# Attention and feed-forward in one kernel: the builder's slack for work between score pairs halved

## Chip, cores, metric

One core of a Trainium2 chip. The metric is the device time of one execution in microseconds, the median of several.

## The reference, cut to what matters

```python
x = A_x                                            # 1 x 2048 x 512, bf16
g = sigmoid((x * gate_w).sum(-1, keepdims=True))
a = attention(x, wqkv, wo)                         # 32 heads of 16: softmax(q k^T / 4) v, then @ wo
b = (silu(x @ w_gate) * (x @ w_up)) @ w_down       # feed-forward, inner width 1792
return g * a + (1 - g) * b
```

## The kernel before

The attention scores need 32 x 2048 x 2048 exponentials. They are made in tiles of 128 x 512 ("scores"). Most go in pairs: two TensorE matmuls fill one of two PSUM buffers `s_t`, ScalarE's exponential reads both at once and writes `e_t`. In 72 blocks of four, VectorE computes the exponential instead (`d_t` to `y_t` and on). Between two pairs, TensorE does other work in a "gap": output groups (probabilities times values: `o_ps`, or `x_ps` for VectorE's late blocks), and side pieces of two matmuls each (projections `qp`, `kp`, `vp`, feed-forward `gp`, `up`, `dps`, final projection `a_ps`).

The order on every engine is fixed when the kernel is built, by a loop that keeps a model clock for each engine (`plan.pe`, `plan.act`, `plan.dve`). Cut to what matters, with comments added:

```python
def emit_pair(bs):                       # one score pair and its exponential
    ...
    spend("R", 1 if (bs[0] - bs[1]) % 2 else 2, s_end[i])        # 0.216 us, after s_end
    act(out=e_t[:], in_=s_t[:], func=ACT.Exp, scale=inv_sqrt_dh)
    plan.act = max(plan.act, plan.pe + 0.27) + 0.905
    s_end[i] = plan.act + 0.18           # this buffer is free again
    ...
def spend(mode, mms, ready=0.0):         # 0.1 us for a change of matmul mode
    plan.pe = max(plan.pe + (0.1 if mode != plan.mode else 0.0), ready) + (0.226 if mode == "F" else 0.216) * mms
    plan.mode = mode

def side(most):                          # the next side piece, if it fits
    ...
    if t is None or t > plan.pe + 0.1 or 0.226 * mms + (0.1 if plan.mode != "F" else 0.0) > most:
        return None
    return c

SLACK = 0.2
...
while nxt < nb:
    ...
    room = s_end[pairs[0] % 2] - plan.pe             # until the next pair's buffer is free
    if room > 0.02:
        if to_vector() and not d_wait and d_end[0] <= plan.pe + 0.05:
            ...                                      # a d_t score for VectorE goes first
        n_pv = pvs_ready(plan.pe)
        switch = 0.0 if plan.mode == "C" else 0.1
        fits = int((room + SLACK - switch) / 0.216)  # how many output groups fit
        crowded = pairs[0] - min(e_left.values(), default=pairs[0]) >= EB - 4
        c = side(room + SLACK)
        if n_pv and fits > 0 and (plan.mode == "C" or n_pv > 1 and fits > 1 and (pv_turn[0] or c is None)
                                  or crowded or c is None and fits == 1):
            emit_pv(); ...; continue
        if c is not None:
            pace.credit -= emit_piece(c); ...; continue
    ...
    emit_pair(list(range(nxt, min(nxt + 2, nb))))
    nxt += 2
```

A VectorE block's output group counts as ready 0.4 us after the model clock says that the block ends (`late.append((plan.dve + 0.4, mine))`).

Of the kernel before, what the change touches and what calls it, by code (L numbers as in the profile page):

```python
# [78 lines left out]
def kernel(  # L79
# [995 lines left out]
    def side(most):  # L1075

        due = any(not c.out() for n in range(plan.slot, plan.slot + 12) for c in need.get(n, []))
        c = pace.next(plan.slot) if pace.credit > 0 or due else None
        if c is None:
            return None  # L1080
        mms, _, takes = c.pieces[c.i]
        t = m_ready() if takes else 0.0
# [3 lines that stand above are left out]
# [3 lines left out]
            pay_v() if vops else pay_d() if d_wait else pay()  # L1089
        emit_pv()  # L1090

    SLACK = 0.2
    def to_vector():

        un, at_ = divmod(nxt, 4 * KT)
        if vcur:
            if nxt % 4 in [b % 4 for b in vcur["b"]]:
                return 0
            return 2 if at_ >= 4 * KT - 4 * (NV - vcur["i"]) else 1
        if nxt < 16 or at_ > (50 if un < UNITS - 1 else 12) or y_live[0] >= 3 or sum(v[0] for v in vops) > 6:  # L1100
            return 0
        return 1

    while nxt < nb:
# [12 lines left out]
        if room > 0.02:  # L1117
# [6 lines left out]
            switch = 0.0 if plan.mode == "C" else 0.1  # L1124
            fits = int((room + SLACK - switch) / 0.216)
# [3 lines that stand above are left out]
# [105 lines left out]
```

## Time and profile before

| | before |
|---|---|
| median time | 872.0 us |
| span in the profile | 869.8 us |
| ScalarE, TensorE, VectorE busy | 97%, 92%, 92% |
| exponentials on ScalarE | 880, mean record 1.09 us |
| score tiles on VectorE | 288 |

ScalarE is the bound. A **start pitch** is the distance between the starts of two exponentials that follow one another with nothing between; there are 822 such pairs among 880 exponentials. An **end pitch** is the distance between their ends, start plus duration of the record. "Excess" is the sum of what lies over the commonest pitch.

### The profile page before, as it was taken

Reading aid. Unit: us, or ns where it says so; the run is one execution under the profiler, and the core shown is the slowest. Engines: PE = TensorE matmul, PEld = TensorE weight load, DVE = VectorE, ACT = ScalarE, POOL = GpSimd, SP = SyncE. Lnnn points to the kernel's source line nnn. Section 1 sums busy time; section 2 is a strip of 40 time slices with the busy share of each in tenths; the row PEclk is TensorE's granted clock in tenths of the full one; section 3 lists DMA queues with packets and bytes.
Section 4 is the critical chain, followed back from the end, with each engine's and each line's share of the span. In section 5 each row is a group of like instructions: output and inputs, shape, how many; then the busy total and the mean of one; then the engine's idle time right before and its main releaser. Section 6 shows DMA issues by size and latency. Waiting matters only on the chain.

```text
span 869.8 us, 14419 instructions
## 1 busy us (share of the span) xinstructions
PE 798.7 (92%) x5232; PEld 208.8 (24%) x5232; DVE 796.5 (92%) x1117; ACT 842.7 (97%) x944; POOL 8.6 (1%) x31
## 2 busy tenths in 40 slices
PE   5999999999999999999999989989998989889985
PEld 2222222222222222222222222222222222222221
DVE  7889999999999999999999999989999999998974
ACT  3999999999999999999999999999999999999995
POOL 3000000000000000000000000000000000000000
PEclk9999999999999999999999999999999999999999
DMA  8400011111210012211000122110001121100000
GB/s 200 122 1 10 11 38 43 37 41 35 60 31 8 10 42 66 56 50 41 4 6 18 41 49 61 50 35 13 7 17 41 36 61 36 28 10 4 5 20 25
DMA packets 88064, 31.99 MB, mean 37 GB/s; under 512 B 75648, under 2 KB 87544, under 8 KB 87992
## 3 DMA queue, kind: packets, MB, share of 16 engines
q1 hardware_dynamic: 86408, 30.87, 14.5%
q8 instruction: 41, 0.67, 0.3%
q10 hardware_dynamic: 1584, 0.20, 0.1%
q14 instruction: 31, 0.25, 0.1%
HBM read 20.83 MB, written 2.34 MB: 27 GB/s over the span
## 4 chain that ended last, share of the span: by engine, by line
PE 46%; ACT 35%; DVE 8%; issue 8%; SPq 1%; DMA 1%; DVEq 0%; ACTq 0%
ACT e_t L161 33%; PE s_t L158 17%; PE o_ps L158 9%; PE dps L158 5%; PE d_t L158 4%; DVE y_t L167 4%; PE gp L158 3%; ACT th L161 3%; PE up L158 2%; DVE u_t L167 2%; PE a_ps L158 1%; PE qp L158 1%; PE vp L158 1%; PE kp L158 1%; PE x_ps L158 1%
## 5 line engine op out<-in xcount | busy, mean ns | idle before, releaser
L161 ACT ACTIVATE e_t<-s_t 128x1024 bf16<-128x1024 f32 x880 | 819.6, 1090 | 5.4 <-PE s_t L158 4.8
L158 PE MATMUL s_t<-qx,kaug 64*128 64x512 bf16 x1648 | 326.7, 384 | 47.7 <-ACT e_t L161 44.6
L167 DVE TENSOR_SCALAR y_t<-d_t 128x512 uint16<-128x512 f32 x288 | 197.8, 687 | 28.3 <-PE d_t L158 24.5
L158 PEld LDWEIGHTS <-kaug 64*128 64x128 bf16 x2048 | 99.6, 93 | 377.4 <-issue 374.3
L158 PE MATMUL o_ps<-e_t,vaug 128*32 128x512 bf16 x1760 | 172.0, 387 | 0.7 <-ACT e_t L161 0.7
L158 PE MATMUL d_t<-qx,kaug 64*128 64x512 bf16 x272 | 102.5, 377 | 0.6 <-DVE y_t L167 0.6
L167 DVE TENSOR_TENSOR y_t<-y_t,u_t 128x2048 uint16<-128x2048 uint16 x72 | 87.8, 1219 | 1.0
L167 DVE TENSOR_TENSOR u_t<-u_t 128x2048 f16<-128x2048 f16 x72 | 87.6, 1217 | 0.7
L167 DVE TENSOR_TENSOR u_t<-u_t,z_t 128x2048 f16<-128x2048 f16 x72 | 87.6, 1217 | 0.4
L158 PEld LDWEIGHTS <-vaug 128*32 128x32 bf16 x2048 | 45.1, 94 | 133.1 <-issue 130.2
L158 PE MATMUL dps<-wd_t,mt 128*128 128x512 bf16 x224 | 67.8, 384 | 0.0
L158 PE MATMUL gp<-xT,wg 128*128 128x512 bf16 x224 | 67.8, 384 | 0.0
L158 PE MATMUL up<-xT,wu 128*128 128x512 bf16 x224 | 64.7, 383 | 0.0
L167 DVE TENSOR_SCALAR y_t<-y_t 128x2048 uint16<-128x2048 uint16 x72 | 49.5, 688 | 1.2
L167 DVE TENSOR_SCALAR u_t<-z_t 128x2048 f16<-128x2048 uint16 x72 | 49.5, 687 | 0.8
L167 DVE TENSOR_SCALAR z_t<-y_t 128x2048 uint16<-128x2048 uint16 x72 | 49.3, 684 | 0.2
L167 DVE SCALAR_TENSOR_TENSOR mt<-gs,up 128x512 bf16<-128x512 bf16 x56 | 38.2, 682 | 4.7 <-PE up L158 3.4
L167 DVE SCALAR_TENSOR_TENSOR gs<-th,gp 128x512 bf16<-128x512 bf16 x56 | 38.2, 682 | 2.6 <-ACT th L161 2.3
L161 ACT ACTIVATE th<-gp 128x512 bf16<-128x512 f32 x56 | 36.7, 655 | 0.0
L158 PEld LDWEIGHTS <-mt 128*128 128x128 bf16 x263 | 16.2, 99 | 43.2 <-issue 35.1
L158 PE MATMUL s_t<-on,kaug 64*128 64x512 bf16 x112 | 22.4, 383 | 1.8 <-ACT e_t L161 1.4
L158 PEld LDWEIGHTS <-wu 128*128 128x128 bf16 x224 | 14.2, 97 | 30.1 <-issue 24.7
(104 smaller groups left out, 358.0 us busy)
## 6 DMA issues: line engine op xcount, KB each, us to landing
wg<-in_B_w_gate_dram SPq DMA_DIRECT2D x56, 128.0 KB
wu<-in_B_w_up_dram SPq DMA_DIRECT2D x56, 128.0 KB
on<-osb SPq DMA_DIRECT2D x120, 16.0 KB
rb<-rr SPq DMA_DIRECT2D x15, 128.0 KB
wd_t<-in_B_w_down_dram SPq DMA_DIRECT2D x1, 1792.0 KB
qx<-qst SPq DMA_DIRECT2D x112, 16.0 KB
out_dram<-o_t SPq DMA_DIRECT2D x12, 128.0 KB
kaug<-on SPq DMA_DIRECT2D x20, 64.0 KB
```

What stands on the lines that cost most here:

```text
L158: ordered(nc.tensor.matmul(*args, **kw))
L161: ordered(nc.scalar.activation(*args, **kw))
L167: return lambda *a, **kw: ordered(f(*a, **kw))
```

## The change

So far a side piece and an output group could share one gap and overrun it. The intent is to stop that: work may pass the moment at which the next score buffer is free only by what still leaves the next exponential on time.

```diff
-    SLACK = 0.2
+    SLACK = 0.1
     def to_vector():
```

## The prediction

> **What bounds the kernel now.** I read the page first: busy shares, then the costliest groups.
>
> ```profile
> PE 798.7 (92%) x5232; PEld 208.8 (24%) x5232; DVE 796.5 (92%) x1117; ACT 842.7 (97%) x944; POOL 8.6 (1%) x31
> ...
> L161 ACT ACTIVATE e_t<-s_t 128x1024 bf16<-128x1024 f32 x880 | 819.6, 1090 | 5.4 <-PE s_t L158 4.8
> L158 PE MATMUL s_t<-qx,kaug 64*128 64x512 bf16 x1648 | 326.7, 384 | 47.7 <-ACT e_t L161 44.6
> L167 DVE TENSOR_SCALAR y_t<-d_t 128x512 uint16<-128x512 f32 x288 | 197.8, 687 | 28.3 <-PE d_t L158 24.5
> ```
>
> ScalarE is the bound: 880 exponentials, each over one pair of score matmuls, 97% busy with only 5.4 us of visible idle in front of them. TensorE is nearly as full, but 44.6 us of its idle is a wait for an exponential to free a score buffer (there are two): it has room. The other part of the softmax, 288 single score tiles (d_t), is exponentiated on VectorE in 72 blocks of four.
>
> 97% looks like nothing is left, but an exponential's record lasts 1.09 us on average and 880 of them fill only 819.6 us, 0.93 each: the records overlap. So an exponential can start up to 0.18 us late with no idle shown. I therefore went to the timeline, at a place where one gap between two score pairs holds a side piece (two gp matmuls, one step of the feed-forward part) and an output group (o_ps, probabilities times values). First TensorE alone:
>
> ```profile
> 643.32 0.39 PE L158 MATMUL s_t<-qx,kaug 64*128 64x512 bf16 x2
> 644.20 0.39 PE L158 MATMUL s_t<-qx,kaug 64*128 64x512 bf16 x2 [0.49 <-ACT e_t L161]
> 644.52 0.60 PE L158 MATMUL gp<-xT,wg 128*128 128x512 bf16 x2
> 645.06 0.40 PE L158 MATMUL o_ps<-e_t,vaug 128*32 128x512 bf16 x3
> 645.39 0.39 PE L158 MATMUL s_t<-qx,kaug 64*128 64x512 bf16 x2
> 645.71 0.60 PE L158 MATMUL gp<-xT,wg 128*128 128x512 bf16 x2
> 646.25 0.39 PE L158 MATMUL s_t<-qx,kaug 64*128 64x512 bf16 x2
> ```
>
> Then ScalarE over the same stretch, three narrow windows:
>
> ```profile
> 643.97 1.09 ACT L161 ACTIVATE e_t<-s_t 128x1024 bf16<-128x1024 f32 x1
> ```
> ```profile
> 644.88 1.10 ACT L161 ACTIVATE e_t<-s_t 128x1024 bf16<-128x1024 f32 x1
> ```
> ```profile
> 645.88 1.02 ACT L161 ACTIVATE e_t<-s_t 128x1024 bf16<-128x1024 f32 x1
> ```
>
> Starts 643.97, 644.88, 645.88: the pitch is 0.91, then 1.00. The exponential fed by the pair at 645.39 started 0.49 after that pair, 0.1 late, and its record still overlaps the one before (644.88 + 1.10 = 645.98). That lateness is what the change is after, and the waits do not list it.
>
> **How much of it there is.** I went through the whole trace in the same way: for each exponential, its distance from the one before, and what TensorE did between the two score pairs. Where no other activation lies between (822 of 879), the commonest distance is 0.903 us, and never less. Everything above 0.903, summed, is 19.9 us: all that perfect feeding could gain. By content of the gap (output groups, side pieces, d = a d_t score):
>
> ```
> gap holds            gaps  mean pitch ns  over 925 ns  excess us
> side + 1 group         48      1042            40         6.7
> side + 2 groups        13      1000             6         1.3
> d + 2 groups           55       947            32         2.4
> d + side               73       922            24         1.4
> 3 groups               18       996             8         1.7
> 2 side pieces          21       946             7         0.9
> one side              243       911             2         1.9
> 2 groups              106       910             2         0.7
> d + 1 group           106       909             1         0.6
> nothing / d alone  77/ 40   907/916             0/1       0.8
> ```
>
> Eleven pitches reach 1.2 us (stalls behind VectorE, not late feeding); single excesses over 0.3 us are 1.8 of the 6.7 us in the first row and about 6 us overall.
>
> **What the Trainium skill says.** (1) "Perfetto Trace Analysis", section Optimizing Scalar/DVE Operations: ScalarE pays about 51 ns per instruction on PSUM; with 0.833 ns per element from "ScalarE: Activation LUTs", section What ACT_TABLE_LOAD costs, 1024 elements make an estimate of 853 + 51 = 904 ns. The trace agrees: 903. So 0.903 is a floor that this change cannot move. (2) "TensorEngine Tiling (Array Packing)", section Key Properties: changing the tiling mode drains TensorE. Scores run in 64-row mode, output groups in 32-column mode, side pieces in full mode. Agrees: pair to side takes 0.32 (644.20 to 644.52), the side's two matmuls and the next switch 0.54, group and switch 0.33. (3) "TensorE: Matmul & The Clock Gate", section Back-to-back issue gap: about 216 ns for 512 columns; so each of those steps is matmuls at 0.216 plus about 0.1 for a switch. The change saves switches on an engine that isn't the bound.
>
> **The change part by part.** Only the instruction order changes; the kernel's builder runs a model clock, and SLACK says how far past the moment at which the next score buffer falls free (its s_end) work may run.
>
> How late may a pair be? In the trace the earliest pair starts about 0.05 us after the end of the exponential two before. The shortest pair-start to exponential-start is 0.49. Two pitches are 1.806; minus the record of 1.085 and minus 0.49 leaves 0.23 after that end, 0.18 after the earliest start. So a gap is free up to a pair-to-pair time of 0.903 + 0.18 = 1.08. Contents, with the steps above: side 0.86; two groups 0.87; three groups, d + side and d + two groups all about 1.08, on the edge; side + group 1.19, late by 0.11. The rows of the table follow this.
>
> In the builder's figures: after a pair the room is 0.905 - 0.216 = 0.689; a side with its switch takes 0.552 and leaves 0.137; a group with a switch needs 0.316. 0.137 + 0.2 admits it, 0.137 + 0.1 does not. Third groups (0.157 + slack against 0.216) and d + side (0.473 + slack against 0.552) pass with 0.1 too, but only where the pair before was on time; with 0.2 they also pass behind a late pair. A shared gap stays only where the room is long (after one of the 56 tanh activations).
>
> Removed: (a) shared gaps, 6.7 less the 1.8 us of large stalls: 4.8 us. (b) half of the small excess of side + two groups (0.8) and of two sides (0.9): 0.8 us. (c) a third of the small excess of d + two groups (1.9), d + side (1.4), three groups (0.3): 1.2 us; the others stay, being admitted still. Together 6.8 us.
>
> Added: about 60 to 70 groups move to other gaps, in twos, some 30 gaps. 117 gaps are empty or hold a d alone. A two-group gap costs 7 ns over the floor, 0.2 us in all; some 20 become edge gaps at 30 ns, 0.6 us. One more microsecond for groups forced out when the ring of 12 exponential tiles fills and for chance collisions with VectorE. Together 1.8 us.
>
> Sum: 872.0 - 6.8 + 1.8 = **867.0 us**, 0.6% faster.
>
> **The rivals.**
> 1. TensorE hasn't the gaps: unsharing makes a backlog and groups are forced out late in the ring's last moment. For it: TensorE is 95.9% busy between 200 and 400 us, and waits for exponentials just 112 times. Against it: that busy share contains about 0.1 of switch per step, of which unsharing saves one per gap, and in each 100 us there are 8 to 18 gaps empty or with d alone against 5 to 13 shared. If half the groups came out late by about 0.2 us, 6 us would be lost again: 872 to 875.
> 2. VectorE takes fewer blocks: the builder gives it a score tile when its clock is free, and its own work is 92% busy. A shorter run has less VectorE time; one block fewer means two more exponentials, 1.8 us. For it: a saving of 6 us is most of one block's time (on the page's durations 4 x 0.69 + 3 x 0.69 + 3 x 1.22 = 8.5 us). Against it: VectorE waits 24.5 us for d_t scores, and those get into a gap first. One or two blocks fewer: 869 to 871; one more: 865.
> 3. The lateness costs nothing, because something else ends the run. For it: just 5.4 us of ScalarE idle is shown. Against it: ScalarE is in an unbroken row from 18 to 860 us and nothing catches up a late start. Time then: 872.
>
> **Range and chances.** The mechanism is counted, so the centre lies near the sum; rivals 1 and 2 pull upward by 2 to 5 us, and a full success of all the removable small excess (13 us less what stays at the edge) would give 863. Range 862.8 to 871.0. To be faster by 2% takes 17.4 us of the 19.9 in existence, stalls included: 1%. Slower by 2% takes a backlog much beyond rival 1: 2%. Within 2%: 97%.
>
> **What would show it right or wrong.** Right: side + group gaps fall from 55 (7 of them beside a tanh) to under 10; pitches over 925 ns from 127 to under 70; excess over 0.903 from 19.9 to about 15 us; still 880 exponentials, give or take 4; matmul counts unchanged; the wait of s_t for e_t rises above 46 us. Wrong: shared gaps gone but as many late pitches with three groups or d + two groups (rival 1); 882 or 884 exponentials and fewer than 288 d_t conversions (rival 2); pitches shorter but the same span (rival 3). Large VectorE stalls that shift by chance, 6 us in all, are the largest thing that I can't compute.

## The result, and the profile after

The changed kernel takes 868.99 us (867.87 to 870.62, 4 runs) against 872.01 us (871.86 to 873.24, 4 runs). The ratio is 0.9964, 95% interval 0.9944 to 0.9984: 0.36% faster, within the 2% that counts as the same. (A ratio is the mean of one kernel's fast runs over the mean of the other's in the same rounds, so not quite the ratio of the medians.) The time lies in the predicted range; the gain is 3.0 us where 5.0 was forecast.

The page after, the lines that answer those shown of before:

```profile
PE 789.8 (91%) x5145; PEld 217.3 (25%) x5232; DVE 797.3 (92%) x1120; ACT 842.4 (97%) x944; POOL 8.6 (1%) x31
...
L161 ACT ACTIVATE e_t<-s_t 128x1024 bf16<-128x1024 f32 x880 | 823.3, 1143 | 3.2 <-PE s_t L158 2.4
L158 PE MATMUL s_t<-qx,kaug 64*128 64x512 bf16 x1648 | 332.2, 384 | 43.6 <-ACT e_t L161 38.3
L167 DVE TENSOR_SCALAR y_t<-d_t 128x512 uint16<-128x512 f32 x288 | 198.0, 687 | 30.7 <-PE d_t L158 26.9
```

The same instructions: 880 exponentials, 288 tiles on VectorE (87 of 5232 matmul records are missing from this trace; the second profile of the same kernel, below, has all). The surprise is in the exponentials' line. An exponential's record now lasts 1.143 us, where it was 1.090. The exponential did not become slower: more of them ran closely one behind the other. Counted from the two traces, gap by gap:

```
                                     before   after
gaps with one side + one group           55       2
start pitches over 925 ns               127     121
excess of starts over 0.903 us         19.9    17.4
  of which side + one group             6.7     0.0
           d + side                     1.4     3.9
           d + two groups               2.4     3.4
           two groups                   0.7     2.2
           three groups                 1.7     1.9
excess of ends over 0.917 us            7.5     5.0
  of which single ones over 0.1 us      6.9     4.6   (20 and 19 of them)
```

So the shared gaps went, as predicted, and their 6.7 us with them, and yet hardly fewer starts are late: other rows grew. The time follows the last part of the table, not the first.

**Why ends and not starts.** Take the prediction's own three ScalarE lines. The starts are 643.97, 644.88 and 645.88, and the third seems 0.1 late. But the ends are 643.97 + 1.09 = 645.06, 644.88 + 1.10 = 645.98 and 645.88 + 1.02 = 646.90: 0.92 apart, both times. The late start cost nothing. Its record is just shorter. The kernel after shows the other half of it, in five narrow windows of ScalarE's timeline; each line is two overlapping exponentials, with the start of the first and the time to the end of the second:

```profile
588.17 2.09 ACT L161 ACTIVATE e_t<-s_t 128x1024 bf16<-128x1024 f32 x2
```
```profile
589.08 2.10 ACT L161 ACTIVATE e_t<-s_t 128x1024 bf16<-128x1024 f32 x2
```
```profile
589.98 2.12 ACT L161 ACTIVATE e_t<-s_t 128x1024 bf16<-128x1024 f32 x2
```
```profile
590.88 2.13 ACT L161 ACTIVATE e_t<-s_t 128x1024 bf16<-128x1024 f32 x2
```
```profile
591.79 2.14 ACT L161 ACTIVATE e_t<-s_t 128x1024 bf16<-128x1024 f32 x2
```

Starts: 0.91, 0.90, 0.90, 0.91 apart. Ends (590.26, 591.18, 592.10, 593.01, 593.93): 0.92 apart. Over the trace of before, 537 starts on time stand 0.9033 us apart on average while their ends stand 0.9167 apart (915 to 918 ns for nine in ten), and each record is 0.013 us longer than the one before it. A record that follows idle time is 1.018 us long; the longest is 1.258 us here and 1.316 in the kernel after. So starts run ahead of the work by up to 0.3 us, and whatever a record has over 1.018 us is a store: a late start draws on it first, and only what goes beyond is lost. The traces bear this out gap by gap. Of the 131 starts of before that are over 0.02 us late, 68 are late by less than the record before them has in store: 3.8 us of lateness in sum, and none of their ends is more than 0.002 us late. In the kernel after it is 93 of 125, 6.8 us of lateness, again at no cost. ScalarE's floor for these exponentials is 0.917 us, not 0.903.

By ends, all that better feeding could still gain in the kernel before was 7.5 us, nearly all of it in 20 stalls of over 0.1 us. The difference in the traces adds up: the spans differ by 1.9 us (869.8 and 867.9), the excess of ends by 2.5, and the first exponential came 0.65 later in this profile of after.

### The profile page after: what moved, and what is told of

Its sections match the earlier page's. It is cut to its first block, busy times and chain, and to the rows that moved or that the text cites. A ratio compares the mean times of both kernels' runs of the same rounds, so it can differ in the third digit from the quotient of the medians.

```text
span 867.9 us, 14339 instructions
## 1 busy us (share of the span) xinstructions
PE 789.8 (91%) x5145; PEld 217.3 (25%) x5232; DVE 797.3 (92%) x1120; ACT 842.4 (97%) x944; POOL 8.6 (1%) x31
## 4 chain that ended last, share of the span: by engine, by line
ACT 40%; PE 38%; DVE 10%; issue 9%; SPq 1%; DMA 1%; DVEq 0%; ACTq 0%
ACT e_t L161 37%; PE s_t L158 15%; PE o_ps L158 7%; PE d_t L158 4%; DVE y_t L167 4%; PE dps L158 3%; ACT th L161 3%; PE gp L158 3%; DVE u_t L167 3%; PE up L158 2%; PE vp L158 1%; PE kp L158 1%; DVE mt L167 1%; PE x_ps L158 1%; SPq L174 1%
## 5 line engine op out<-in xcount | busy, mean ns | idle before, releaser
L158 PE MATMUL s_t<-qx,kaug 64*128 64x512 bf16 x1648 | 332.2, 384 | 43.6 <-ACT e_t L161 38.3
L158 PEld LDWEIGHTS <-kaug 64*128 64x128 bf16 x2048 | 109.4, 93 | 381.2 <-issue 377.3
L158 PE MATMUL dps<-wd_t,mt 128*128 128x512 bf16 x205 | 63.5, 384 | 2.5 <-issue 2.5
L158 PE MATMUL gp<-xT,wg 128*128 128x512 bf16 x202 | 62.9, 384 | 2.4 <-issue 2.4
L158 PE MATMUL up<-xT,wu 128*128 128x512 bf16 x205 | 60.9, 383 | 2.1 <-issue 2.1
L161 ACT ACTIVATE th<-gp 128x512 bf16<-128x512 f32 x56 | 40.7, 727 | 0.0
L167 DVE TENSOR_TENSOR osb<-of,x_ps 128x512 bf16<-128x512 f32 x30 | 20.4, 680 | 1.2 <-PE x_ps L158 1.2
```

Of the source, the lines that this page charges most:

```text
L158: ordered(nc.tensor.matmul(*args, **kw))
L161: ordered(nc.scalar.activation(*args, **kw))
L167: return lambda *a, **kw: ordered(f(*a, **kw))
```

## The experiments

Twelve runs were made, on three chips; the times of the kernel before were 872.26 (7 runs), 872.16 (9) and 872.05 (7). Two theories after the result: **starts** (each late start is lost, as predicted) and **stalls** (the floor is 0.917 by ends; what costs are the few stalls that outrun the store, most of them, it says, with TensorE waiting in order for VectorE).

### Half of each side piece dropped, order kept

```diff
 # gate/up, and in the same way the q, k, v, down and final projections
-                for dc in (2 * h, 2 * h + 1):
+                for dc in (0 if h == 0 else DC - 1,):
                     mm(ps[:, :], lhsT=w[:, dc, :], ...)
```

Their outputs are wrong, which doesn't matter for the times. Once on the kernel before:

> The kernel before with half of the matmuls of each side piece dropped (one 512-column matmul left of two; wrong result on purpose), the order of what remains and the builder's model clock untouched. A side piece then takes about 0.22 us less, so a gap with side and group takes about 0.97 and no pair is late. Theory 1 (the prediction's): ScalarE's floor is the start-to-start pitch of 0.903 us and each late start is lost; then some 13 to 14 of the 19.9 us of excess go and the time is 858 to 860. Theory 2: the floor is the end-to-end pitch of 0.917 us (the records grow by 0.013 per exponential while starts are on time, and shrink again at a late start); then only 7.5 us lay above the floor, almost all in 20 large stalls, and the time is 865 to 869, with records of exponentials longer than before (over 1.15 us on average).

and once on the changed one:

> The same dropping of matmuls in the changed kernel (SLACK 0.1). Theory 1: the same 858 to 860 as the thinned kernel before. Theory 2: 864 to 868, i.e. at the most 5 us under the changed kernel; the two thinned kernels differ by less than 2 us, as feeding is no longer in question.

Measured: 870.94 us (868.32 to 872.81; ratio to before 0.9984, interval 0.9962 to 1.0006) and 872.47 us (870.82 to 873.53; 1.0008, 0.9991 to 1.0024). The starts theory wanted 858 to 860 and is refuted. The stalls theory was also too low: 865 to 869 and 864 to 868. TensorE certainly got its room; on the thinned kernel before:

```profile
PE s_t L158 <- ACT e_t L161: 104.9, 332, 1.0
```

It waits 104.9 us for exponentials (before: 46.0). In 702 of 878 cases the pair starts within 0.06 us of its buffer coming free (before: 307), and the records average 1.181 us, but ends stay 0.917 apart. That is the floor, shown with feeding out of the way. What remains over it, 6.8 us, sits where it sat before: stalls at 145.7, 277, 411.9, 460.1, 555.7, 670.4, 682.3, 825.8 us, the same places to 1 us as in the kernel before, most of them smaller. The rest of the miss is new: this profile has three 3.4 us windows at half TensorE clock inside the exponentials (the other: four), where before had one; 2.6 us (3.9 us) of the excess lies in them or just behind. The thinned TensorE was busy for 84% and 85% of the span instead of 92%, and its clock was lowered more often (mean granted clock 0.993 and 0.991, before 0.996). That the one brings the other is not shown, but it confounds these two runs' times, not their floor.

### Slack 0.1 for one kind of work alone

```diff
-            fits = int((room + SLACK - switch) / 0.216)
+            fits = int((room + 0.1 - switch) / 0.216)        # groups_only
-            c = side(room + SLACK)
+            c = side(room + 0.1)                             # sides_only
```

> Slack 0.1 for output groups alone, 0.2 still for side pieces. Side and group then share no short gap. Theory 1: the shared gaps were 4.8 of the 6.8 us to be had, so this is most of the change: 868 to 869.5. Theory 2: small lateness was free, only which large stalls happen to occur matters: anywhere from 867 to 873, without order between the variants of slack, and the excess of ends over 0.917 explains the time to within 0.5 us.

Measured: 870.67 us, ratio 0.9982 (0.9967 to 0.9997). Gaps with one side and one group: 5 beside no tanh (48 before). So with the shared gaps gone the time falls by 0.2%, less than the starts theory wanted; it looks like about half of the change's gain, but the interval overlaps that of the changed kernel (0.9954 to 0.9984). The excess of ends is 5.4 us, 2.1 less than before; the first exponential came 1.4 us later, and the spans differ by 0.7 us, so the ends account for it.

> Slack 0.1 for side pieces alone, 0.2 for output groups. Behind a side a group is again admitted, so shared gaps stay near before's; the builder's TensorE clock ends 3.3 us past ScalarE's, so some pieces are left for the end. Tail 2 to 3 us longer, 872 to 875; the gain of the change is not in this half.

Measured: 881.23 us (1.0104, 1.0083 to 1.0125), 6 us over what was expected. The tail after the last exponential is 12.4 us as foreseen (9.7 before), but the excess of ends doubled to 15.0 us: shared gaps rose (88 without a tanh), side pieces fell behind, and six stalls of over 1 us appeared (the kernel before has none); among TensorE's waits is one for a bound that stands behind its projection on VectorE (`bp` for `aq`, three times, 3.3 us). So the slack for side pieces alone did harm, and the gain does not lie in this half alone.

### The changed kernel again

> The changed kernel once more, for the scatter between chips and to see whether its large stalls sit at the same places: 868 to 870.5. If they are properties of the order (VectorE behind the builder's clock), most of the stalls over 0.1 us of the first profile are there again within 1 us of the same time; if they are chance, they are elsewhere.

Measured: 868.99 us, ratio 0.9969 (0.9954 to 0.9984). It was run at another time. Its stalls stand where the first profile had them: 247, 278, 287, 371, 500, 603, 724, 752, 817 us, within about 1 us and of the same size. So most stalls belong to the order of instructions, not to chance. An exception is one of 1.45 us at 21.6 us, inside a half-clock window that the first profile did not have; the first had four in or behind a half-clock window at 843 us instead, 1.4 us together. That the excess of ends is 4.99 us here and 4.98 there is therefore partly luck.

What makes these stalls is still a VectorE block's output group in half of the cases. One of them in this profile:

```profile
286.22 0.40 PE L158 MATMUL x_ps<-y_t,vaug 128*32 128x512 bf16 x4 [0.52 <-DVE y_t L167]
...
286.76 0.39 PE L158 MATMUL s_t<-qx,kaug 64*128 64x512 bf16 x2
...
287.26 1.02 ACT L161 ACTIVATE e_t<-s_t 128x1024 bf16<-128x1024 f32 x1 [0.32 <-PE s_t L158]
```

Counted in the traces: in the kernel before, the gap just ahead of the late pair holds such a group in 8 of the 20 stalls, 3.8 of their 6.9 us; here in 8 of 16, 2.1 of 4.6 us. TensorE waits for `y_t` before such groups as long as it did (3.1 and 3.0 us in sum), but less of it reaches ScalarE.

The wait of score pairs for exponentials is 38.9 us in this complete trace: it fell from 46.0, where the prediction had it rise.

### VectorE made faster, order kept

```diff
-                (1.26, lambda: vec.tensor_tensor(out=ua, in0=ua, in1=ua, op=ALU.mult)),
+                (1.26, lambda: vec.tensor_tensor(out=uh, in0=uh, in1=uh, op=ALU.mult)),   # 1024 columns of 2048
 # and the same for the two that follow
```

> The kernel before, every engine's instruction order unchanged, but the three 2048-column multiplications and additions of each VectorE block cover 1024 columns (wrong result on purpose): VectorE has some 1.8 us less work per block, TensorE and ScalarE the same. Theory V (the time above ScalarE's floor lies in the stalls in which TensorE, in order, waits for a VectorE block, a gated product or a d_t buffer; five of the largest in the profile of before, 0.43 to 0.85 us, show such a wait just ahead): these stalls go, the excess of ends over 0.917 falls from 7.5 to under 3.5 us, the time is 867 to 868.5. Theory F (late feeding by TensorE itself is what costs): no change, 871.5 to 873.

Measured: 870.12 us, ratio 0.9977 (0.9965 to 0.999). (The result, wrong, still passed the comparison.) Between the two theories. The excess of ends is still some 6.6 us, where under 3.5 was expected, because a half-clock window at 19.9 us, which the profile of before does not have, brings 1.9 us. Outside half-clock windows it fell from 6.4 to 3.6 us; the stalls at 461, 671 and 825 us are gone. Those at 147.7, 414.4, 557.3 and 683.7 us remain, and their lines say why. First the kernel before, all engines:

```profile
144.12 0.69 DVE L167 TENSOR_SCALAR y_t<-y_t 128x2048 uint16<-128x2048 uint16 x1
...
144.86 0.40 PE L158 MATMUL o_ps<-y_t,vaug 128*32 128x512 bf16 x4 [0.47 <-DVE y_t L167]
145.19 0.39 PE L158 MATMUL s_t<-qx,kaug 64*128 64x512 bf16 x2
...
145.68 1.02 ACT L161 ACTIVATE e_t<-s_t 128x1024 bf16<-128x1024 f32 x1 [0.44 <-PE s_t L158]
```

TensorE stands before a VectorE block's output group; the next score pair is behind it in the queue, and ScalarE runs dry. Then the same place with the faster VectorE:

```profile
145.49 0.69 DVE L167 CAST on<-kp 128x512 bf16<-128x512 f32 x1 [2.10 <-PE kp L158]
...
146.09 0.68 DVE L167 TENSOR_SCALAR y_t<-y_t 128x2048 uint16<-128x2048 uint16 x1
...
146.83 0.40 PE L158 MATMUL o_ps<-y_t,vaug 128*32 128x512 bf16 x4 [0.47 <-DVE y_t L167]
147.16 0.39 PE L158 MATMUL s_t<-qx,kaug 64*128 64x512 bf16 x2
...
147.66 1.02 ACT L161 ACTIVATE e_t<-s_t 128x1024 bf16<-128x1024 f32 x1 [0.44 <-PE s_t L158]
```

VectorE now sits idle for 2.10 us before a copy of `kp`, for which it waits on TensorE; the last step of the block is queued behind that copy; TensorE waits for the block. This stall is made by the order on two engines, and the faster VectorE did not remove it. In sum VectorE's speed explains part of the stalls (2.8 us); such an interlock is shown for this one, and the other three have a VectorE block's group just ahead of the late pair too.

### A later ready time for VectorE's blocks

```diff
-                                late.append((plan.dve + 0.4, mine)))),
+                                late.append((plan.dve + 1.0, mine)))),
```

> Slack 0.2 as before, but the builder takes the output group of a VectorE block as ready 1.0 us after its model clock instead of 0.4. Theory V: TensorE no longer waits at o_ps or x_ps for y_t, 868 to 870.5, with a correct result and without touching the shared gaps (some 50 still there). Theory F: no gain, 871.5 to 873.

> Slack 0.1 and the ready time of 1.0 us together. Theory V: waits for y_t gone here too, 866.5 to 869, and the difference to slack 0.2 with the same ready time is under 1.5 us. Theory F: the same time as the changed kernel, 869, and 3 us under slack 0.2.

Measured: 869.91 us at slack 0.2 (0.9969, 0.9957 to 0.9982), 870.05 us at slack 0.1 (0.9975, 0.9961 to 0.9989). At slack 0.2 most of the change's gain appears with its shared gaps all still there (72 of any kind, before 67). So a gain of this size does not need the shared gaps to go. (That it was not theirs in the change is read from their ends, below.) The two gains do not add: slack 0.1 with the later time is no faster than either alone. The waits for `y_t` did not vanish, as I had expected, but went from 2.5 and 0.6 us (`o_ps`, `x_ps`) to 1.3 and 0.4 us at slack 0.2. In the changed kernel they are 0.7 and 2.3 us, no less in sum, so shorter waits are not how the change gained.

### ScalarE's clock in the builder corrected

```diff
-        plan.act = max(plan.act, plan.pe + 0.27) + 0.905
-        s_end[i] = plan.act + 0.18
+        plan.act = max(plan.act + 0.917, plan.pe + 1.288)
+        s_end[i] = plan.act + 0.05
 # e_end, tanh and its reader in the same way; SLACK 0.15
```

> The builder's ScalarE clock as the profile shows it: an end follows an end by 0.917 us, or a pair's issue end by 1.288 us; a score buffer is free 0.05 us after the end; slack 0.15. The builder then lays 73 VectorE blocks and 878 exponentials instead of 72 and 880. Two exponentials fewer are 1.8 us. If the floor of ends is right: 866 to 870; if the floor of starts were right, the builder would leave ScalarE waiting and the time would be over 873.

Measured: 869.1 us, ratio 0.9965 (0.9952 to 0.9977), 878 exponentials. The floor is two exponentials lower, but the excess of ends is 6.6 us: the new order has stalls of its own. No faster than the change.

### Other values of slack

> Slack 0.15, 880 exponentials, nothing left for the end. Late feeding theory: between before and after, 870 to 871. Stalls theory: anywhere in 868 to 872, with the excess of ends over 0.917 and the number of half-clock windows telling where; sub-0.1 us excesses of ends sum to under 1 us as in all kernels so far.

> Slack 0.3, 878 exponentials (73 blocks), nothing left for the end. More late starts than in any kernel so far, start excess over 25 us. Late feeding theory: 876 or more. Stalls theory: late starts of up to about 0.2 us use up ScalarE's overlap first, but with so many the overlap runs out and part of each is paid: 870 to 874, records of exponentials shorter on average than 1.09 us.

> Slack 0.05. The builder's own end state has 73 VectorE blocks (878 exponentials) and TensorE's model clock 8.5 us past ScalarE's, where the changed kernel has 0.4: side pieces no longer fit the gaps and are left for the end. Theory R (the prediction's first rival, met one step of slack further on): the exponentials end a little earlier than in the changed kernel, the tail after the last one grows from 9.7 to about 17 us, time 873 to 877. If small lateness were what counts, fewer late starts would make it faster than 869.

| slack | time | ratio to before (95%) | late starts | excess of ends | outside half-clock windows | mean record |
|---|---|---|---|---|---|---|
| 0.05 | 895.84 | 1.027 (1.0243 to 1.0296) | 100 | 22.9 | 8.1 | 1.172 |
| 0.10 (after again) | 868.99 | 0.9969 (0.9954 to 0.9984) | 119 | 5.0 | 3.4 | 1.144 |
| 0.15 | 872.15 | 1.0005 (0.9979 to 1.003) | 119 | 8.6 | 3.4 | 1.125 |
| 0.20 (before) | 872.0 | | 127 | 7.5 | 6.4 | 1.089 |
| 0.30 (878 exponentials) | 871.93 | 1.0002 (0.9981 to 1.0024) | 156 | 8.8 | 8.8 | 1.064 |

The ratio is to the kernel before. Kernels are compared only within the same rounds. The profile of 0.05 is of its fastest execution, that of 0.15 of its slowest (874.94). Three things are to be read here. First, at **0.30** the store is used up: the records are 1.064 us on average, 70 ends are over 20 ns late (before: 30), and small lateness begins to cost. My expectation of over 25 us excess of starts was wrong (20.9).

(A stall that ends in or just behind a half-clock window is counted to the windows even where the same wait brought the window on: 6.4 us at 0.05 and 2.1 us at 0.15 are such.)

Second, the median of **0.15** is not between 0.1 and 0.2 but before's, though its interval (0.9979 to 1.003) does not exclude the middle. In its profile, one wait of TensorE, behind a 2.28 us maximum over keys on VectorE:

```profile
135.45 0.62 PE L158 MATMUL x_ps<-y_t,vaug 128*32 128x512 bf16 x4 [1.96 <-DVE ge L167]
```

and the busy times of the stretches around it (columns: length, then PE, PEld, DVE, ACT, POOL busy, granted clock, DMA share, GB/s):

```profile
127.40:130.80 3.40, 3.40 (x22) 0.87 (x21) 3.40 (x6) 3.40 (x5) 0.00 (x0) 1.00 0.10 14
130.80:134.20 3.40, 2.45 (x26) 1.03 (x25) 3.26 (x5) 3.40 (x5) 0.00 (x0) 1.00 0.57 101
134.20:141.00 6.80, 5.55 (x28) 1.18 (x27) 5.95 (x10) 3.45 (x4) 0.00 (x0) 0.50 0.20 42
```

The wait begins at 133.5. At 134.2, after a stretch with TensorE busy for 2.45 of 3.40 us, its clock is halved for 6.8 us, and ScalarE is busy for only half of them (3.45). So a stall of 2.1 us became 4.0 (the ends of 136.7 to 141.3 us). Its fastest run, 870.47, had the highest mean clock (0.997), its slowest, 874.94, the lowest (0.989).

Third, **0.05** is a cliff, of the kind that the prediction's first rival named: work that comes out late. The waits of ScalarE in the kernel before, and then at slack 0.05:

```profile
ACT e_t L161 <- PE s_t L158: 4.8, 11, 0.7
ACT scaled L161 <- PE a_l L158: 3.5, 1, 3.5
```
```profile
ACT e_t L161 <- PE s_t L158: 20.1, 17, 6.2
ACT scaled L161 <- PE a_l L158: 11.0, 1, 11.0
```

The second line is the tail: 7.5 us more TensorE work left after the last exponential. The first contains one stall of 6.2 us, which the chain of work that ended last resolves:

```profile
191.08 1.04 PE kp L158 x4
192.12 0.02 issue
192.14 0.70 DVE on L167
192.84 0.02 issue
192.87 2.30 DVE kb L167
...
195.47 0.59 PE bp L158
196.06 0.96 PE s_t L158 x3
```

A key projection comes out in one row, as the builder lays work whose deadline has come (its `force`), and everything that depends on it (copy, 2.30 us of maximum, bound) follows with nothing else between; the clock is halved from 194.8 us on, for 10 us. By the builder's figures, a side piece behind a d_t score needs 0.552 in a room of 0.473: admitted at slack 0.1, refused at 0.05. So are two groups behind a d_t score (0.532). In the traces gaps with d + side fall from 93 to 69, those with d + two groups from 49 to 14. That these refusals starved the projections is likely but was not tested. I had expected the tail, 873 to 877, not the forced pieces.

### Where the 2.8 us come from

Outside half-clock windows, sorted by how late the start is over 0.903 ("store" is the mean of the previous record over 1.018):

```
                start late by      gaps   starts us   ends us   store us
before          0.02 to 0.10        72       3.8        0.3      0.098
                0.10 to 0.25        41       6.1        1.3      0.117
                over 0.25           11       5.9        4.8      0.092
after           0.02 to 0.10        68       3.7        0.1      0.155
                0.10 to 0.25        37       5.2        1.0      0.180
                over 0.25           11       4.3        2.6      0.151
after again     0.02 to 0.10        70       3.9        0.1      0.157
                0.10 to 0.25        35       4.8        0.8      0.184
                over 0.25           11       4.4        2.6      0.151
```

In total 6.4, 3.6 and 3.4 us of ends. The small class was nearly free already. In the large class, 11 stalls against 11: starts are 1.6 us less late in sum, because the stalls of the new order are other ones; and each meets a store that is 0.06 us larger, 0.6 us in sum. The middle and small classes give 0.6 us more. So some 1.2 us of the gain are fewer small losses and a better cushion, which would follow from the change's intent (starts that are on time build the store), and 1.6 us are shorter stalls in this order. That split is worked out from two orders; whether another order at slack 0.1 would keep the second part is open, and the runs with a later ready time (4.2 us at 0.2, 4.0 us at 0.1) suggest that it would not.

No version tried beats the change: 868.99 twice, 869.1 (clock corrected) and 869.91 (later ready time) are not separated by their intervals.

## Why the prediction was right or wrong

- **Range, direction, class: right, in good part by luck.** 868.99 in 862.8 to 871.0; 3.0 us of gain for 5.0. The cost that the prediction meant to remove was hardly a cost, and the gain came mostly from stalls that it had left out of its sum.
- **ScalarE is the bound and this change cannot touch its floor: right, but the floor was wrong.** The step "0.903 us, and never less: everything above, summed, is 19.9 us" took starts for throughput. The ends show 0.917, and only 7.5 us to be had. That an estimate from the skill's figures gave 904 made me stop looking.
- **"Nothing catches up a late start": wrong, and the term that it mis-sized is (a).** Of the 48 shared gaps, 44 were late by 4.6 us in starts; their ends cost 0.36 us. The other 1.7 us of ends are four stalls. (a) was put at 4.8 us.
- **Shared gaps vanish: right** (55 to 2; under 10 predicted). **Late pitches from 127 to under 70: wrong** (121). With a larger store the exponentials before a pair end later in relation to their starts, so the same edge gaps would show as late more often (argued, not tested): d + side over 925 ns from 24 of 73 to 43 of 84. These are not costs (0.3 to 0.5 us of ends).
- **Terms (b) and (c), 2.0 us: not in the rows named.** The gain that is there comes from stalls of over 0.1 us, which the prediction had set aside as what it couldn't compute. It said so, and rightly; but it then took them as unchanged.
- **Added, 1.8 us:** not seen as such. The rows to which the groups moved grew in starts (two groups from 0.7 to 2.2 us), but most of that was absorbed, and what is left can't be told from the stalls.
- **Rival 1 (no gaps): false here, true in kind at 0.05,** which takes 24 us more. The large stalls there stand behind projections or what depends on them (`bp`, `qx`), so side pieces rather than the groups that the rival named. The prediction saw the margin in empty gaps, not how near the room of a d + side gap was.
- **Rival 2 (fewer blocks): false,** 72 blocks. **Rival 3 (lateness costs nothing): dismissed, and for small lateness its outcome was the true one.** Its reason was not: nothing else ends the run, ScalarE's own work by ends does. Its evidence, 5.4 us of visible idle, was closer to the 7.5 us than my 19.9.

## What to carry to other kernels

Where an engine's records overlap, measure its floor by their ends as well as by their starts: here records grew while starts were punctual, which meant work in store, and a late start was a loss only by what went beyond that store. Before tuning small lateness on the bound engine, list the few stalls that outrun that store, and see which engine's queue order made them; in two profiles of this static order most stood within about 1 us of the same place. When a slack in a scheduler is tightened, look for the piece of work that will no longer fit anywhere: at 0.1 no such pile-up showed, at 0.05 projections came out late in a row, and the kernel took 24 us more.

## What the Trainium skill lacked or had wrong

- "ScalarE: Activation LUTs", section What ACT_TABLE_LOAD costs, says that back-to-back ACTIVATEs overlap by about 93 ns. Here the overlap is not one number: a record is 1.018 us after idle time and grows by 0.013 us per punctual exponential to over 1.3, with starts 0.903 and ends 0.917 us apart. No page has this growth, or says that late starts draw on it.
- "Perfetto Trace Analysis", section Optimizing Scalar/DVE Operations: the estimate from its 51 ns, 904 ns for 1024 elements from PSUM, meets the start pitch (903) and is 13 ns under the sustained rate (917).
- "TensorE: Matmul & The Clock Gate", Part 1, has the half clock come after an idle window of about 3.4 us. Here it came behind 3.4 us that were far from idle, with TensorE busy for 2.45 us in the run with slack 0.15, 2.09 in the thinned kernel before (501.5 to 504.9) and 1.83 in the kernel before (839.7 to 843.1), and it lasted 3.4 to 10 us. (At slack 0.05, ahead of 194.8 us, TensorE was busy for only 0.70.) A later section of that part does tie it to frequent short idles, but no page says how busy is busy enough.
